# The last 96 hidden features of an MLP on Trainium2, computed as three strips of 32 in TensorE's column groups and row groups

## The chip, the cores and the metric

The kernel runs on one core of a Trainium2 chip. The metric is the time of one execution in microseconds of device time, lower is better. Engines are named as in the profile: PE is TensorE (matrix multiply; PEld is its loading of weights), DVE is VectorE, ACT is ScalarE, POOL is GpSimd, SP is SyncE, which here only issues DMAs.

## The reference

Four layers follow one another on x of 2048 tokens by 512 features, bfloat16: a long-convolution layer A, an MLP B, and both again with the same weights.

```
x = A_q
x = x + A(layernorm(x))
x = x + B(layernorm(x))
x = x + A(layernorm(x))
x = x + B(layernorm(x))

A(q) = q * (causal_conv(kv, ssm_k) + kv * ssm_D)     # kv = shift(k) * v, by FFT of length 4096
B(x) = gelu(layernorm(x) @ w1 + b1) @ w2 + b2        # w1 is 512 x 1376, w2 is 1376 x 512
```

The factor that multiplies q in A depends on k and v alone, so it is the same for both A layers and is computed once. The hidden width is F = 1376 = 10 x 128 + 96.

## The kernel before

**Two parts.** The first part of the program (to about 100 us) computes the factor of A by Fourier transforms written as matmuls, and in its last stretch begins the MLP of the first four token tiles. Its pieces stand in an order written out by hand, the string `ORDER`: each word is the name of a piece, the engine that takes it (P, D, A, G for GpSimd, S for SyncE's DMAs) and the slots it uses. `_Plan.write` emits the pieces in that order. The second part (from about 101 us to the end) is a loop written in plain code, each engine taking its instructions in the order in which they are emitted.

**The loop.** The 2048 tokens are 16 tiles of 128, in 4 groups of `GT = 4` tiles (512 tokens). The loop takes n = 0 to 7: groups 0 to 3 for the first MLP and 0 to 3 again for the second. For each n:

- `mm1(n)` makes the hidden activations `hT`, features on partitions, 512 tokens along the free axis. For each of `FT = 11` feature tiles, 4 matmuls (one for each 128 of the 512 inputs, `ct`) add up in a PSUM buffer `ph` of pool `ps2`, and ACT applies gelu with the bias `B1` into `hT`. The last feature tile has only `FL = 96` features.
- `mm2(n)` multiplies back: for each token tile i, 11 matmuls of 512 columns (one for each feature tile) add up in an accumulator `po` of pool `ps3`. The eleventh contracts over 97 rows: 96 features and a row of ones, which meets b2 in a 97th row of the weights `W2t`. The first two token tiles stop after 8 feature tiles and are finished later, so that ACT has time for the last gelus.
- `done(i)` on DVE adds the accumulator to the tokens `x_t`; for n of 4 and more the result is sent out.
- `prep(n + 2)`, two turns ahead, has four steps on DVE, two of which end with one small POOL instruction (`scale`): `c0` statistics of the first layernorm (POOL: `scale`), `c1` the normalised tokens times the factor of A, added to `x_t`, `c2` statistics of the next norm (POOL: `scale`), `c3` the norm applied into `lnx`, and a transposing DMA on SP from `lnx` into `lnT[n % 3]`, from which `mm1(n + 2)` reads. `c0` and `c1` are emitted ahead of `mm1(n)`, `c2` after the first 16 matmuls of `mm2(n)`, `c3` after `done(1)`.

For n = 0 the hidden activations are made within the hand-written order, by the pieces `M0a` to `M2c` (token tiles 0, then 1, then 2 and 3 together), and `prep(1)` and `prep(2)` both run beside `mm2(0)`.

**Memory.** One big tile, `arena`, holds nearly all data; `place` gives each array an offset in it, and arrays that live at different times share a place. `Ft` holds the table of the first transform stage. The dependency tracking of the framework puts in the waits.

Of the kernel before, what the change touches and what calls it, by code (L numbers as in the profile page):

```python
# [18 lines left out]
lSK.S wm2.P2 bS.P2 wm0.P1 bSe.A dg0.D dg1.A dg2.A lk0.S lk1.S lh1.S kT0.P2 bSK.P1 bSKe.A kT0e.D kT1.P0 kT2.P3 lh113.S lb1.S lx0.S kT1e.D kT2e.A kT3.P1 wm1.P0 bB.P2 bBe.A lv0.S s00.A lv1.S kT3e.D kv10.P3 kvm10.D kv00.P1 U1S0.P30 kv01.P2 kvm00.D U1S1.P1 U0S0.P01 U1S0e.D lK01.S kg0.G kv11.P3 lK00.S kg1.G U0S0e.A kvm01.D U0S1.P0 s01.G U0S1e.A U0S3.P2 U1S1e.D kvm11.D U0S3e.A kv20.P1 kd0.P0 lK11.S lK10.S kvm20.D kd0e.A U1S3.P3 U0S2.P2 U1S3e.A U0S2e.D KS11.P0 KS11e.A KS01.P1 KS30.P3 KS01e.A lW.S KS00.P2 KS00e.A KS30e.D KS10.P0 KS31.P1 KS10e.D kv21.P3 kvm21.D KS31e.A kd4.P1 kd4e.A KS20.P0 KS21.P2 KS20e.A KS70.P1 KS21e.D KS51.P3 KS41.P0 KS70e.A KS51e.A KS60.P2 KS60e.A KS41e.D KS40.P1 KS61.P3 KS40e.D lX.S KS71.P0 KS50.P2 U1S2.P1 KS71e.D KS61e.A KS50e.A U1S2e.A U2S0.P32 U2S0e.D K25.P0 K25e.A K27.P2 K24.P1 K24e.A K23.P3 K21.P0 K21e.A K27e.D K26.P2 U2S1.P1 K26e.A K23e.D U2S1e.D K20.P3 K28.P0 K20e.A K22.P2 K22e.A K212.P1 K28e.D K215.P3 K215e.A lM.S K212e.D sa1.S sb1.S sa0.S K214.P0 K29.P2 K29e.A K213.P1 U0T0.P3 K214e.D K213e.A K210.P0 K210e.A sb0.S K211.P2 U0T1.P1 s02.D K211e.A U2S3.P0 U0T0e.D U2S3e.A U0T1e.D ka1.G kg2.G ka2.G kg3.G X00.P30 ka3.G kgm.G U3S0.P21 U3S0e.D U2S2.P1 X00e.A X01.P01 lH.S U2S2e.A U1T0.P3 U3S1.P2 T00.D0 U3S3.P1 X01e.A U1T1.P0 sb3.S U1T0e.D X10.P30 U3S1e.A U3S3e.A sa3.S X02.P22 T01.D1 X10e.A U2T0.P1 sb2.S U1T1e.D T10.D2 U3S2.P3 U2T0e.D X02e.A sa2.S X12.P01 V00.P2 U3S2e.A T02.D0 V10.P30 X12e.A X03.P10 V00e.A X03e.A V01.P0 V01e.A X20.P22 T12.D2 X20e.A U3T0.S V12.P1 X11.P01 X11e.A V10e.D lx.S V02.P3 U2T1.P2 T03.D1 X13.P00 T20.D2 V12e.A V02e.A T11.D0 V03.P1 U2T1e.D X13e.A V03e.A X30.P32 T13.D1 V11.P0 X30e.A V11e.D X23.P21 V13.P1 X23e.A U3T1.S V13e.A T30.D0 X22.P30 X22e.A T23.D1 V20.P01 X21.P22 ly.S X21e.A V20e.A V30.P12 X32.P31 T22.D2 T21.D0 X31.P20 V22.P0 X32e.A V21.P3 X31e.A V30e.D X33.P12 V22e.A Z01.S Z00.S X33e.A V23.P2 T32.D2 V23e.A T31.D0 V32.P0 V31.P1 T33b.D1 V33b.P2 T33a.D2 V31e.D Z11.S Z10.S V21e.A V32e.A V33a.P3 Z03.S V33ae.A TC0a.P0 TC0b.P1 Z13.S TC0ae.A TC0be.A w4.S V33be.D TD0b.P3 TD0a.P0 TD0ae.D TC3.P2 TD0be.A Y00.P0 Y01.P3 Y00e.A Y01e.A TC3e.D g00.D w1.S Z02.S TC1.P1 TC1e.A g01.D h00.D Y02.P2 Y32.P0 TC2.P3 Y02e.A h01.D Y32e.A Y10.P1 Y10e.A p00.G w3.S b00.D g02.D p01.G LT0.P2 LT0e.A Y12.P0 Y12e.A M0b.P1 M0be.A TC2e.A h02.D M0a.P2 b01.D LT1.P1 Y30.P0 LT1e.A p02.G b02.D LT2.P3 LG1.D LT2e.D M1a.P1 M0ae.A M1ae.A M1b.P2 M1be.A M2a.P3 M2ae.A M2b.P1 M2be.A M2c.P2 M2ce.A Y30e.A Z12.S w2.S Y20.P3 Y22.P1 Y20e.A Y22e.A  # L19
# [85 lines left out]
def kernel(ctx: ExitStack, tc: tile.TileContext, A_q, A_k, A_v, A_shift_k, A_ssm_k, A_ssm_D,  # L105
# [9 lines left out]
    FL = F - (FT - 1) * P  # L115
    TOK = "(p nt) d -> p nt d"
# [58 lines left out]
    B1 = const.tile([P, FT], F32, name="B1")  # L175
# [88 lines left out]
    W2t = place("W2t", [P, FT, D], 75 * K)  # L264
# [3 lines left out]
    hT = place("hT", [P, FT, GT * P], 0)  # L268
    lnT = [place(f"lnT{i}", [P, GT, CT, P], o * K) for i, o in enumerate((12, 16, 20))]
    lnx = [place(f"lnx{i}", [P, GT, D], (96 + 4 * i) * K) for i in range(2)]  # L270
    tmpa = place("tmpa", [P, GT, D], 28 * K)
    ZV = at(100 * K, [[1, 8 * D]])

    with tc.tile_pool(name="ps", bufs=1, space=bass.MemoryType.PSUM) as ps:
# [93 lines left out]
        def bias(o):  # L368
            for ft in range(FT):
                nc.tensor.matmul(o[:, ft:ft + 1], b1r[:, ft * P:ft * P + P], one[0:1, 0:1], start=True, stop=True)  # L370
        _, sb = mm_evac("bB", 650, lS[1:2], bias, [FT], lambda: B1[:])
# [314 lines left out]
        def head(n, part, f0, f9, deps):  # L686
            a, b = UNITS[n]
            w = (b - a) * P

            def rows(ft):  # L690
                return P if ft < FT - 1 else FL

            def mms(it):
                o = view(pf[it["slot"]["ps"]], [f9 - f0, w])
                for ft in range(f0, f9):
                    m = rows(ft)
                    for ct in range(CT):
                        nc.tensor.matmul(o[0:m, ft - f0, :].rearrange("p (i t) -> p i t", t=P), W1t[:, ct, ft * P:ft * P + m],  # L698
                                         lnT[0][:, a:b, ct, :], start=ct == 0, stop=ct == CT - 1)
            pe = plan.add(f"M{n}{part}", {"P": 218 * (b - a) * (f9 - f0)}, deps, mms, take=["ps"])  # L700

            def gelu(it):
                o = view(pf[pe["slot"]["ps"]], [f9 - f0, w])
                for ft in range(f0, f9):
                    m = rows(ft)
                    nc.scalar.activation(hT[0:m, ft, a * P:b * P], o[0:m, ft - f0, :], AF.Gelu_apprx_tanh, bias=B1[0:m, ft:ft + 1])
# [18 lines left out]
    with tc.tile_pool(name="ps2", bufs=4, space=bass.MemoryType.PSUM, reuse_waits="tile") as ps2, \  # L725
            tc.tile_pool(name="ps3", bufs=4, space=bass.MemoryType.PSUM, reuse_waits="tile") as ps3:

        def mm1(n, a=0, b=GT, f0=0, f9=FT):
            lt = lnT[n % 3]
            for ft in range(f0, f9):  # L730
                m = P if ft < FT - 1 else FL
                ph = ps2.tile([P, GT * P], F32, name="ph", tag="ph")
                o = ph[0:m, a * P:b * P]
                for ct in range(CT):
                    nc.tensor.matmul(o.rearrange("p (i t) -> p i t", t=P), W1t[:, ct, ft * P:ft * P + m], lt[:, a:b, ct, :],  # L735
                                     start=ct == 0, stop=ct == CT - 1)
                nc.scalar.activation(hT[0:m, ft, a * P:b * P], o, AF.Gelu_apprx_tanh, bias=B1[0:m, ft:ft + 1])  # L737

        def prep(n):
# [19 lines left out]
            def c3():  # L759
                L.apply(ln, g, 0, GT)  # L760
                nc.sync.dma_start_transpose(lnT[n % 3].rearrange("p i ct t -> p (i ct) t"),
                                            ln.rearrange("p i d -> p (i d)"))
            return [c0, c1, c2, c3]

        def mm2(n, g, last, between):
            def part(i, po, f0, f9, a=0, b=D):
                for ft in range(f0, f9):
                    m = P if ft < FT - 1 else FL + 1
                    nc.tensor.matmul(po[:, a:b], hT[0:m, ft, i * P:(i + 1) * P], W2t[0:m, ft, a:b],  # L769
                                     start=ft == 0, stop=ft == FT - 1)  # L770

            def done(i, po, a=0, b=D):
                xs = x_t[:, GT * g + i, a:b]
                nc.vector.tensor_tensor(xs, po[:, a:b], xs, ALU.add)  # L774
# [10 lines left out]
            part(0, po0, FT - 3, FT)  # L785
            done(0, po0)
            part(1, po1, FT - 3, FT)
            done(1, po1)
            for f in between[1:]:
                f()  # L790
            po2 = acc()
            part(2, po2, 0, FT)
            done(2, po2)
            if n < 2 * NG - 1:
                po3 = acc()
                part(3, po3, 0, FT)
                done(3, po3)
            else:
                for a in (0, D // 2):
                    po3 = acc()  # L800
                    part(3, po3, 0, FT, a, a + D // 2)
                    done(3, po3, a, a + D // 2)

        NG = NT // GT
        with tc.manual_schedule(engines={ENG.PE, ENG.DVE, ENG.Activation, ENG.Pool, ENG.SP}):
            nc.gpsimd.memset(hT[FL:FL + 1, FT - 1, :], 1.0)
            for n in range(2 * NG):
# [8 lines left out]
                LG[1].scale(0, GT)  # L816
                for f in one_[1:] + pr[:1]:
                    f()
# [31 lines left out]
```

## Time and profile before

| | before |
|---|---|
| time, median of 3 runs | 249.34 us (249.3 to 249.93) |
| time of the profiled execution | 249.34 us |
| span of its profile, first to last instruction | 247.6 us |
| mean granted TensorE clock | 0.997 |
| PE busy | 236.1 us, 95% of the span, 1918 matmuls |
| DVE busy | 171.9 us, 69% |
| ACT busy | 145.1 us, 59% |
| POOL busy | 54.5 us, 22%, 50 instructions |

The profile has a page (busy times, the span in 40 slices, the chain of work that ended last, groups of instructions by line) and views that can be asked of its trace: the timeline of an engine, the instructions of one line, the waits, the engines' busy time in given stretches. The duration of a matmul in these rows includes its way through the array; successive matmuls overlap, so what a matmul costs in a stream is read from the distance between starts. In a form such as "128\*96 128x512" the first pair is rows and columns of the array that the weights fill, the second is the moving operand: 128 partitions by 512 columns.

### The profile page before, as it was taken

To read this page: it belongs to the slowest core of one execution; us is meant where nothing else is said; L and a number is where in the kernel's file an instruction comes from. 1 tells how busy PE (TensorE), PEld (TensorE's weight loads), DVE (VectorE), ACT (ScalarE), POOL (GpSimd) and SP (SyncE) were. 2 spreads that over 40 slices of the span, in tenths; PEclk is the share of its full clock that TensorE was granted. 3 is DMA by queue.
4 is the path that set the end of the run, shared out by engine and by line. 5 is a ranking of instruction groups with operands and counts; after the bars stand their busy time and mean duration, and the time that the engine had idled before them with its cause. 6 is when DMAs were issued, how large, how long until landed. Compare 5 with 4: busy or idle time off the path is not lost.

```text
span 247.6 us, 4783 instructions
## 1 busy us (share of the span) xinstructions
PE 236.1 (95%) x1918; PEld 146.4 (59%) x1929; DVE 171.9 (69%) x315; ACT 145.1 (59%) x218; POOL 54.5 (22%) x50
## 2 busy tenths in 40 slices
PE   4999999899999999999999999999999999999994
PEld 2689877699998688444444444444444444444443
DVE  1467899999997988878889898956956961021022
ACT  5596899899999899707406506505605604704800
POOL 2789999400000221111101111011011010000000
PEclk9999999999999999999999999999999999999998
DMA  6999994946999990040601204013016016011011
GB/s 244 351 292 173 264 437 192 394 175 120 218 254 179 282 260 5 0 85 1 87 0 38 47 3 85 0 23 63 3 44 127 0 45 127 1 42 42 3 42 42
DMA packets 50816, 29.65 MB, mean 120 GB/s; under 512 B 44675, under 2 KB 48488, under 8 KB 49258
## 3 DMA queue, kind: packets, MB, share of 16 engines
q1 hardware_dynamic: 50642, 29.21, 45.7%
q8 instruction: 15, 0.25, 0.4%
q10 hardware_dynamic: 152, 0.14, 0.2%
q14 instruction: 7, 0.06, 0.1%
HBM read 16.23 MB, written 2.10 MB: 74 GB/s over the span
## 4 chain that ended last, share of the span: by engine, by line
PE 72%; DVE 9%; ACT 9%; DMA 5%; issue 2%; POOL 0%; ACTq 0%; DVEq 0%; POOLq 0%
PE po L769 31%; PE ph L735 27%; ACT arena L215 3%; DMA arena<-in_A_v_dram 3%; ACT xb L215 3%; PE p L521 3%; DVE arena L217 3%; ACT ZT L215 2%; DMA arena<-in_A_ssm_D_dram 2%; PE p L698 2%; PE p L303 2%; DVE arena L254 2%; PE p L403 1%; PE p L335 1%; PE p L575 1%
## 5 line engine op out<-in xcount | busy, mean ns | idle before, releaser
L737 ACT ACTIVATE arena<-ph,B 128x512 bf16<-128x512 f32 (+1 forms) x77 | 52.9, 687 | 78.6 <-PE ph L735 78.6
L769 PE MATMUL po<-arena 128*128 128x512 bf16 (+2 forms) x356 | 77.1, 372 | 0.4
L735 PE MATMUL ph<-arena 128*128 128x512 bf16 (+1 forms) x308 | 67.6, 379 | 0.0
L769 PEld LDWEIGHTS <-arena 128*128 128x128 bf16 (+1 forms) x363 | 35.4, 98 | 40.7
L774 DVE TENSOR_TENSOR arena<-po,arena 128x512 bf16<-128x512 f32 (+1 forms) x33 | 21.6, 672 | 44.6 <-PE po L769 44.5
L735 PEld LDWEIGHTS <-arena 128*128 128x128 bf16 (+1 forms) x308 | 30.8, 100 | 35.9
L215 ACT ACTIVATE arena<-p 128x1024 bf16<-128x1024 f32 (+7 forms) x44 | 40.6, 1005 | 3.6 <-PE p L383 1.2
L249 POOL TENSOR_TENSOR lrsm<-lrsm,mhalf 128x4 f32<-128x4 f32 (+2 forms) x10 | 9.1, 910 | 92.3 <-DVE lrsm L243 89.5
L237 DVE BATCH_NORM_STATS2 lstm<-arena 128x6 f32<-128x512 bf16 x32 | 20.0, 681 | 0.2
L215 ACT ACTIVATE ZT<-p 128x1024 bf16<-128x1024 f32 (+1 forms) x18 | 17.9, 1040 | 1.9 <-PE p L303 1.7
L566 DVE TENSOR_TENSOR T<-xb,arena 128x2048 bf16<-128x2048 bf16 (+1 forms) x17 | 18.9, 1153 | 0.0
L254 DVE TENSOR_SCALAR arena<-arena,lmvg,lrsg 128x512 bf16<-128x512 bf16 x32 | 12.9, 465 | 7.3 <-POOL lrsg L249 7.3
L249 POOL TENSOR_TENSOR lrsg<-lrsg,mhalf 128x4 f32<-128x4 f32 x8 | 8.1, 1012 | 44.6 <-DVE lrsg L246 44.6
L237 DVE BATCH_NORM_STATS2 lstg<-arena 128x6 f32<-128x512 bf16 x28 | 17.2, 677 | 0.0
L575 PE MATMUL p<-arena,T 128*128 128x128 bf16 x256 | 16.2, 219 | 0.6 <-ACT ZT L215 0.3
L215 ACT ACTIVATE xb<-p 128x1024 bf16<-128x1024 f32 x16 | 16.3, 1059 | 0.6 <-PE p L551 0.6
L217 DVE COPY arena<-p 128x2048 bf16<-128x2048 bf16 (+3 forms) x12 | 12.3, 1031 | 5.1 <-PE p L439 3.3
L575 PEld LDWEIGHTS <-T 128*128 128x128 bf16 x256 | 14.8, 98 | 1.1 <-issue 0.7
L453 POOL TENSOR_TENSOR T<-arena,SK 128x2048 bf16<-128x2048 bf16 (+3 forms) x4 | 15.0, 3760 | 1.3 <-ACT SK L215 1.1
L254 DVE TENSOR_SCALAR arena<-arena,lmvm,lrsm 128x512 bf16<-128x512 bf16 x32 | 11.5, 416 | 2.8 <-POOL lrsm L249 2.8
L217 DVE CAST arena<-p 128x1024 bf16<-128x1024 f32 x11 | 12.9, 1217 | 0.3
L217 DVE CAST ZT<-p 128x1024 bf16<-128x1024 f32 (+1 forms) x11 | 12.8, 1170 | 0.4 <-ACT arena L215 0.2
(80 smaller groups left out, 249.5 us busy)
## 6 DMA issues: line engine op xcount, KB each, us to landing
arena<-arena SPq DMA_DIRECT2D x8, 512.0 KB, 5.6
arena<-in_A_k_dram SPq DMA_DIRECT2D x2, 1024.0 KB, 6.2
arena<-in_A_v_dram SPq DMA_DIRECT2D x2, 1024.0 KB
arena<-in_A_ssm_k_dram SPq DMA_DIRECT2D x4, 512.0 KB, 12.1
arena<-tabM SPq DMA_DIRECT2D x1, 2048.0 KB
out_dram<-arena SPq DMA_DIRECT2D x15, 128.0 KB, 1.7
arena<-in_A_q_dram SPq DMA_DIRECT2D x1, 1536.0 KB, 6.8
arena<-in_B_w_dram SPq DMA_DIRECT2D x1, 1376.0 KB, 6.7
```

Of the source, the lines that this page charges most:

```text
L215: nc.scalar.activation(dst, src, AF.Copy)
L217: nc.vector.tensor_copy(dst, src)
L237: nc.vector.bn_stats(self.st[:, i, 0, :], x_t[:, GT * g + i, :] if src is None else src[:, i, :])
L249: nc.gpsimd.tensor_tensor(self.rs[:, a:b], self.rs[:, a:b], mhalf[:, a:b], ALU.pow)
L254: nc.vector.tensor_scalar(out=dst[:, i, :], in0=xs, scalar1=self.mv[:, i, 0:1], scalar2=self.rs[:, i:i + 1], op0=ALU.subtract, op1=ALU.mult)
L453: nc.gpsimd.tensor_tensor(m[:, t:NT, :], kn[:, 0:NT - t, c3], sk(t, NT - t), ALU.mult)
L566: eng.tensor_tensor(view(Tb[it["slot"]["T"]], [2, n, CW]), x2, kk, ALU.mult)
L575: nc.tensor.matmul(o[:, i, :], T[:, r, i, :], Mt[:, ka + i, 1 - r, :], start=r == 0, stop=r == 1)
L735: nc.tensor.matmul(o.rearrange("p (i t) -> p i t", t=P), W1t[:, ct, ft * P:ft * P + m], lt[:, a:b, ct, :], start=ct == 0, stop=ct == CT - 1)
L737: nc.scalar.activation(hT[0:m, ft, a * P:b * P], o, AF.Gelu_apprx_tanh, bias=B1[0:m, ft:ft + 1])
L769: nc.tensor.matmul(po[:, a:b], hT[0:m, ft, i * P:(i + 1) * P], W2t[0:m, ft, a:b], start=ft == 0, stop=ft == FT - 1)
L774: nc.vector.tensor_tensor(xs, po[:, a:b], xs, ALU.add)
```

## The change

The 96 hidden features that do not fill a feature tile are taken out of the loops over feature tiles, and cut into `FS = 3` strips of 32 features.

- **First product, `tail_mm`.** For each strip s and each `ct`, four matmuls, one for each token tile i of the group, have the same 32 columns of `W1t` as weights and 128 tokens as moving operand. The result of tile i goes to PSUM partitions 32i to 32i + 31, that is to column group i of the array. So 48 matmuls of 128 columns stand where 4 of 512 columns stood. In the loop they come first in `mm1`, ahead of the ten full feature tiles; for n = 0 they are a new piece `M3` (with `M3e` on ACT) at the end of `ORDER`, after the last products of A.
- **Gelu, `tail_gelu`.** Three ACT instructions of 128 partitions by 128 write `hq`: on partitions 32i to 32i + 31 the strip's features of token tile i. `B1` has 13 columns in place of 11, the last three with each strip's bias repeated four times; they are made by 22 small matmuls in place of 11.
- **Second product, `tail` in `mm2`.** For each strip, four matmuls, one for each token tile, contract over 32 rows: partitions 32i to 32i + 31, that is row group i of the array. They write four accumulators, which are all taken at the start of `mm2`. So 12 matmuls of 512 columns stand where 4 stood (for n = 7 the last tile's accumulator is in two halves). They come after the first 16 matmuls of `mm2`. The weights for them, `W2q`, hold the last 96 rows of w2 four times, once for each group of 32 partitions, loaded by four DMAs where one was.
- **b2.** The row of ones goes, and with it the POOL memset. b2 is loaded into `Ft`, repeated on all partitions, and POOL adds it to `x_t` (`add_b2`): for group 0 in four instructions of 512 columns behind the `scale` of `prep(1)`, for the others in one of 2048 columns at the end of `c3`. The adds are eight groups' worth in all.

At the end of the string `ORDER` stand two words more, `M3.P0 M3e.A`; the rest of it is as before. The diff without that line:

```
+    FS = FL // 32
...
-    B1 = const.tile([P, FT], F32, name="B1")
+    B1 = const.tile([P, FT + FS - 1], F32, name="B1")
...
+    hq = place("hq", [P, FS, P], 10 * K)
+    W2q = place("W2q", [P, FS, D], 136 * K)
     ZV = at(100 * K, [[1, 8 * D]])
+
+    def tail_mm(o, lt):
+        for s in range(FS):
+            f0 = (FT - 1) * P + 32 * s
+            for ct in range(CT):
+                for i in range(GT):
+                    nc.tensor.matmul(o[32 * i:32 * i + 32, s, :], W1t[:, ct, f0:f0 + 32], lt[:, i, ct, :], start=ct == 0, stop=ct == CT - 1)
+
+    def tail_gelu(o):
+        for s in range(FS):
+            nc.scalar.activation(hq[:, s, :], o[:, s, :], AF.Gelu_apprx_tanh, bias=B1[:, FT - 1 + s:FT + s])
...
-            for ft in range(FT):
+            for ft in range(FT - 1):
                 nc.tensor.matmul(o[:, ft:ft + 1], b1r[:, ft * P:ft * P + P], one[0:1, 0:1], start=True, stop=True)
-        _, sb = mm_evac("bB", 650, lS[1:2], bias, [FT], lambda: B1[:])
+            for s in range(FS):
+                f0 = (FT - 1) * P + 32 * s
+                for i in range(GT):
+                    nc.tensor.matmul(o[32 * i:32 * i + 32, FT - 1 + s:FT + s], b1r[:, f0:f0 + 32], one[0:1, 0:1], start=True, stop=True)
+        _, sb = mm_evac("bB", 650, lS[1:2], bias, [FT + FS - 1], lambda: B1[:])
...
-        w3 = load("w3", W2t[0:FL, FT - 1, :], B_w2[(FT - 1) * P:F, :], 96 << 10, wd)
-        w4 = load("w4", W2t[FL:FL + 1, FT - 1, :], apf(B_b2, 0, [[D, 1], [1, D]]), 1024, wd)
+
+        def load_tail(it):
+            for i in range(GT):
+                nc.sync.dma_start(W2q[32 * i:32 * i + 32, :, :], apf(B_w2, (FT - 1) * P * D, [[D, 32], [32 * D, FS], [1, D]]))
+        w3 = plan.add("w3", {"S": 600}, wd, load_tail, dma=("copy", 384 << 10))
+        w4 = load("w4", Ft[:, 0:D], apf(B_b2, 0, [[0, P], [1, D]]), 2 ** 17, wd)
...
-            for part, f0 in enumerate(range(0, FT, step)):
-                head(n, "abc"[part], f0, min(f0 + step, FT), [lt[n], w1])
+            for part, f0 in enumerate(range(0, FT - 1, step)):
+                head(n, "abc"[part], f0, min(f0 + step, FT - 1), [lt[n], w1])
+        m3 = plan.add("M3", {"P": 640}, [lt[n] for n in range(3)] + [w1], lambda it: tail_mm(view(pf[it["slot"]["ps"]], [FS, P]), lnT[0]),
+                      take=["ps"])
+        plan.add("M3e", {"A": 600}, [m3, sb] + wd, lambda it: tail_gelu(view(pf[m3["slot"]["ps"]], [FS, P])), free=[(m3, "ps")])
...
-        def mm1(n, a=0, b=GT, f0=0, f9=FT):
+        def mm1(n):
             lt = lnT[n % 3]
-            for ft in range(f0, f9):
-                m = P if ft < FT - 1 else FL
+            ph = ps2.tile([P, GT * P], F32, name="ph", tag="ph")
+            pt = ph[:, 0:FS * P].rearrange("p (s t) -> p s t", t=P)
+            tail_mm(pt, lt)
+            tail_gelu(pt)
+            for ft in range(FT - 1):
...
+        def add_b2(g, a, b):
+            xs = x_t[:, GT * g + a:GT * g + b, :]
+            b2 = apf(Ft, 0, [[Ft.shape[1], P], [0, b - a], [1, D]])
+            nc.gpsimd.tensor_tensor(xs, xs, b2, ALU.add)
...
                                             ln.rearrange("p i d -> p (i d)"))
+                add_b2(g, 0, GT)
             return [c0, c1, c2, c3]
...
+            def tail(parts):
+                for s in range(FS):
+                    for i, po, a, b in parts:
+                        rs = slice(32 * i, 32 * i + 32)
+                        nc.tensor.matmul(po[:, 0:b - a], hq[rs, s, :], W2q[rs, s, a:b], start=s == 0 and i > 1, stop=False)
...
-            po0, po1 = acc(), acc()
-            part(0, po0, 0, FT - 3)
-            part(1, po1, 0, FT - 3)
+            parts = [(i, acc(), 0, D) for i in range(GT)]
+            if n == 2 * NG - 1:
+                parts[3:] = [(3, parts[3][1], 0, D // 2), (3, ps2.tile([P, GT * P], F32, name="ph", tag="ph"), D // 2, D)]
+            for i, po, *_ in parts[:2]:
+                part(i, po, 0, 8)
             for f in between[:1]:
                 f()
...
+            tail(parts)
+            for i, po, *_ in parts[:2]:
+                part(i, po, 8, FT - 1)
+                done(i, po)
...
-            nc.gpsimd.memset(hT[FL:FL + 1, FT - 1, :], 1.0)
...
                 one_ = prep(1)
                 LG[1].scale(0, GT)
+                for i in range(GT):
+                    add_b2(0, i, i + 1)
                 for f in one_[1:] + pr[:1]:
                     f()
                 mm2(0, 0, False, pr[1:])
```

Two places in the order of instructions matter below. The first is POOL's queue from the last `scale` of the hand-written part on. In these rows `lrsm` and `lrsg` are the scales of the two norms and `mhalf` their exponent; L249 before and L250 after are the same line of `scale`. Before:

```order
L249 TENSOR_TENSOR lrsm0_110<-lrsm0_110,mhalf_77 128x2 [waits DVE_49]
L806 MEMSET arena_64 1x512 [waits DMAHW3_49,Activation_49,Pool_49]
L249 TENSOR_TENSOR lrsg1_107<-lrsg1_107,mhalf_77 128x4 [waits DVE_49,Pool_49]
L249 TENSOR_TENSOR lrsm1_113<-lrsm1_113,mhalf_77 128x4 [waits DVE_49]
L249 TENSOR_TENSOR lrsg0_104<-lrsg0_104,mhalf_77 128x4 [waits DVE_49]
L249 TENSOR_TENSOR lrsm0_110<-lrsm0_110,mhalf_77 128x4 [waits DVE_49]
```

After, where L765 is `add_b2`:

```order
L250 TENSOR_TENSOR lrsm0_110<-lrsm0_110,mhalf_77 128x2 [waits DVE_49]
L250 TENSOR_TENSOR lrsg1_107<-lrsg1_107,mhalf_77 128x4 [waits DVE_49]
L765 TENSOR_TENSOR arena_64<-arena_64,Ft_73 128x512 [waits DMAHW4_49,DMAHW5_49,PE_49,Pool_49]
L765 TENSOR_TENSOR arena_64<-arena_64,Ft_73 128x512 [waits PE_49] x3
L250 TENSOR_TENSOR lrsm1_113<-lrsm1_113,mhalf_77 128x4 [waits DVE_49]
L765 TENSOR_TENSOR arena_64<-arena_64,Ft_73 128x2048 [waits DMAHW6_49,DVE_49,PE_49]
L250 TENSOR_TENSOR lrsg0_104<-lrsg0_104,mhalf_77 128x4 [waits DVE_49]
L250 TENSOR_TENSOR lrsm0_110<-lrsm0_110,mhalf_77 128x4 [waits DVE_49,Pool_49]
```

Four adds now stand right behind the first `lrsg1` scale, which releases `c1` of `prep(1)` on DVE, and ahead of the `lrsm1` scale of its `c2`; one add of 2048 columns stands between that and the `lrsg0` scale of `prep(2)`.

The second place is TensorE's queue in `mm2(1)`, where it comes to the accumulators of token tiles 2 and 3. Before, between the first two tiles' last matmuls and the third tile's first (L769 is the one line of all these matmuls):

```order
L769 LDWEIGHTS arena_64 [waits Activation_49]
L769 MATMUL po_1870<-arena_64 128x512
...
L769 MATMUL po_1871<-arena_64 128x512
L769 LDWEIGHTS arena_64
L769 MATMUL po_1911<-arena_64 128x512 [waits DVE_49]
```

After, from the sixteenth matmul of `mm2(1)` on (L797 is a full feature tile, L804 a strip):

```order
L797 MATMUL po_1980<-arena_64 128x512
L804 LDWEIGHTS arena_64
L804 MATMUL po_1979<-arena_64 128x512
...
L804 MATMUL po_1980<-arena_64 128x512
...
L804 MATMUL po_1981<-arena_64 128x512 [waits DVE_49]
L804 LDWEIGHTS arena_64
L804 MATMUL po_1982<-arena_64 128x512 [waits DVE_49]
```

The first matmul of the third accumulator, with its wait for DVE to have emptied that buffer in the turn before, stood at the 23rd matmul of `mm2`, and now stands at the 19th, the fourth accumulator's at the 20th.

More of the change, by code (lines that the diff above doesn't have):

```diff
@@ L263 @@
     W1t = place("W1t", [P, CT, F], 64 * K)
-    W2t = place("W2t", [P, FT, D], 75 * K)
+    W2t = place("W2t", [P, FT - 1, D], 75 * K)
     KSW = place("KSW", [P, NA, D], 64 * K)
@@ L767, in part @@
                 for ft in range(f0, f9):
-                    m = P if ft < FT - 1 else FL + 1
-                    nc.tensor.matmul(po[:, a:b], hT[0:m, ft, i * P:(i + 1) * P], W2t[0:m, ft, a:b],
-                                     start=ft == 0, stop=ft == FT - 1)
+                    nc.tensor.matmul(po[:, 0:b - a], hT[:, ft, i * P:(i + 1) * P], W2t[:, ft, a:b], start=ft == 0 and i < 2,
+                                     stop=ft == FT - 2)
+            def tail(parts):
[3 more added lines that the diff above has]
+                        nc.tensor.matmul(po[:, 0:b - a], hq[rs, s, :], W2q[rs, s, a:b], start=s == 0 and i > 1, stop=False)
             def done(i, po, a=0, b=D):
                 xs = x_t[:, GT * g + i, a:b]
-                nc.vector.tensor_tensor(xs, po[:, a:b], xs, ALU.add)
+                nc.vector.tensor_tensor(xs, po[:, 0:b - a], xs, ALU.add)
                 if last:
```

36 lines of the change are left out of this document (9 added, 27 removed).

## The prediction

> **What bounds the kernel now.** I read the busy times by stretch first, then the chain that ended last, then the timeline. The stretches (columns: us, then busy us of PE, PEld, DVE, ACT, POOL, with counts) show where the edit lies:
>
> ```profile
> 50.00:88.00 38.00, 36.60 (x548) 33.15 (x548) 36.12 (x43) 36.85 (x42) 1.25 (x2) 1.00 0.94 203
> 101.20:234.71 133.51, 133.14 (x612) 61.08 (x618) 85.70 (x206) 54.91 (x80) 13.10 (x13) 1.00 0.20 40
> ```
>
> From 101.20 us on PE is busy without a gap (133.14 of 133.51 us); DVE, ACT and POOL have room. Earlier, three engines share the bound. The chain in order of time (start, us, what) says the same of the loop:
>
> ```profile
> 101.37 9.51 PE po L769 x44
> 110.88 9.50 PE ph L735 x44
> ```
>
> A turn is 44 matmuls of `mm1` and 44 of `mm2`, 9.50 / 44 = 0.216 us each. So in the loop every us that TensorE gains or loses counts in full, and other engines only if TensorE waits for them.
>
> **TensorE's part.** The matmuls that go are these (columns: busy us, mean ns of one):
>
> ```profile
> L735 PE MATMUL ph<-arena 128*96 128x512 bf16 x28 | 7.2, 379 | 0.0
> L769 PE MATMUL po<-arena 97*128 97x512 bf16 x31 | 11.8, 381 | 0.0
> ```
>
> Per turn that is 4 x 0.216 = 0.86 us in `mm1` and 0.86 in `mm2`. In their place come 48 matmuls of 128 columns and 12 of 512. If four neighbours in different groups run at once, these are 12 rounds of 128 columns and 3 of 512. The trace has no column groups, but it has row groups: the two halves of L403 (64 rows each).
>
> ```profile
> 43.27 0.27 PE L403 MATMUL p<-arena,Wt 64*128 64x256 bf16 x1
> 43.48 1.22 PE L335 MATMUL p<-IDt,ZT 128*128 128x128 bf16 x16
> 44.63 0.28 PE L403 MATMUL p<-arena,Wt 64*128 64x256 bf16 x1
> 44.63 0.39 PE L403 MATMUL p<-arena 64*128 64x256 bf16 x2
> 44.75 0.37 PE L403 MATMUL p<-arena,Wt 64*128 64x256 bf16 x2
> 44.86 0.38 PE L403 MATMUL p<-arena 64*128 64x256 bf16 x2
> 45.61 1.22 PE L335 MATMUL p<-IDt,ZT 128*128 128x128 bf16 x16
> 46.66 0.60 PE L303 MATMUL p<-Ft,arena 128*128 128x256 bf16 x4
> ```
>
> A pair starts at one instant (44.63 twice) and the next 0.11 us later, about what a single matmul of 256 columns takes (L303: (0.60 - 0.27) / 3 = 0.11). Row groups do run at once. The rows also price the change of grouping: L335's 16 full matmuls take 44.63 - 43.48 = 1.15 us where the split L403 follows, 1.05 (46.66 - 45.61) where the full L303 does, so 0.10 us to enter; a pair at 43.27 should be followed at 43.38, and L335 starts at 43.48, so 0.10 to leave. Each tail is entered and left once: 0.20 us per tail, four changes a turn.
>
> `mm2`'s tail, by these rows: 3 x 0.216 + 0.20 = 0.85 us against 0.86, no gain. For `mm1`'s tail I have two rows for its rounds:
>
> ```profile
> 19.08 1.79 PE p L521 x32
> 10.70 0.42 PE L370 MATMUL p<-one,arena 1*128 1x1 bf16 x11
> L370 PE MATMUL p<-one,arena x11: 158/158/173, 10.7 to 11.0; 1*128 1x1 bf16 x11
> ```
>
> L521 streams 128 columns in 1.79 / 32 = 0.056 us, so 12 full rounds are 0.67 us. L370 has next to nothing to stream, and still takes (0.42 - 0.158) / 10 = 0.026 us for a load and a matmul in one group; if that holds across groups, 48 x 0.026 = 1.25 us. With no overlap it is 48 x 0.056 = 2.69. I take 0.67, since L403's pairs start together; that is nearest in kind. Tail: 0.67 + 0.20 = 0.87 against 0.86.
>
> So a turn comes out even: 0.01 x 7 for `mm1`, -0.01 x 8 for `mm2`. For n = 0 it is worse, since `M3` is new work after a stretch that waits for DVE:
>
> ```profile
> 94.68 4.96 PE L698 MATMUL p<-arena 128*128 128x256 bf16 x44 [0.19 <-DVE arena L217]
> ```
>
> What leaves before 94.68 us only lengthens that wait; behind it 4 matmuls of about 0.11 us go, and 0.87 comes: +0.44 us. TensorE's sum is about +0.4 us.
>
> The Trainium skill ("TensorE: Matmul & The Clock Gate", "The mechanism" under Part 3) says that weight loads overlap matmuls in flight only where the row group differs. In `mm1`'s tail every matmul uses all rows; what that would do is a rival below.
>
> **ACT, SP and the bias.** Three gelus of 128 columns replace one of 512:
>
> ```profile
> 91.43 6.76 ACT L706 ACTIVATE arena<-p,B 128x128 bf16<-128x128 f32 x23
> 100.88 2.86 ACT L215 ACTIVATE arena<-p 128x1024 bf16<-128x1024 f32 x3
> ```
>
> 6.76 / 23 = 0.29 each, 0.88 in place of 0.68, beside 8.6 us of matmuls: nothing. For n = 0 ACT ends its evacuations at 103.74, `M3e` at 104.6; `mm2(0)`'s tail comes 16 x 0.216 after 101.2 + 0.44, at 105.1: covered by 0.5 us. Three more loads on SP, 0.57 us each, push the transpose and the big w2 load behind them by 1.7 us:
>
> ```profile
> 82.61 0.57 SPq L279 DMA_DIRECT2D arena<-in_B_w_dram  x1
> 86.17 0.58 SPq L279 DMA_DIRECT2D arena<-in_B_w_dram  x1
> arena<-in_B_w_dram SPq DMA_DIRECT2D x1, 1376.0 KB, 6.7
> ```
>
> w2 then lands near 86.2 + 1.7 + 6.7 = 94.6, needed at 101.2: nothing.
>
> ```profile
> 14.53 2.36 DVE L527 TENSOR_TENSOR arena<-p,arena 128x1024 bf16<-128x1024 f32 x2 [2.90 <-DMA arena<-in_A_v_dram]
> ```
>
> Eleven more 1-column matmuls in the bias, near 11 us, cost 0.3 us and a change of grouping, ahead of a stretch in which DVE, and TensorE behind it, wait for a load until 14.53 us anyway: nothing.
>
> **b2 on POOL.** This is where I expect the loss.
>
> ```profile
> 36.75 0.93 POOL L455 TENSOR_TENSOR T<-kh,SK 128x384 bf16<-128x384 bf16 x1
> 37.75 4.07 POOL L460 TENSOR_TENSOR T<-T,T 128x2048 bf16<-128x2048 bf16 x1
> 41.90 4.09 POOL L464 TENSOR_TENSOR arena<-arena,T 128x2048 bf16<-128x2048 bf16 x1
> 40.53 3.48 DVE L217 CAST arena<-p 128x1024 bf16<-128x1024 f32 x3
> 43.93 3.19 DVE L254 TENSOR_SCALAR arena<-arena,lmvg,lrsg 128x512 bf16<-128x512 bf16 x4
> 95.22 1.38 DVE L254 TENSOR_SCALAR arena<-arena,lmvg,lrsg 128x512 bf16<-128x512 bf16 x4 [0.59 <-POOL lrsg L249]
> 96.63 1.23 DVE L751 TENSOR_TENSOR arena<-arena 128x2048 bf16<-128x2048 bf16 x1
> 97.89 1.23 DVE L752 TENSOR_TENSOR arena<-arena 128x2048 bf16<-128x2048 bf16 x1
> ```
>
> An add of 2048 columns takes 4.07 us, one of 512 between 1.02 (a quarter) and 1.2 (from the 0.93 for 384): I take 1.1. While POOL's L464 ran, DVE's L254 took 3.19 us in place of 1.38: it stood still until POOL ended at 45.99, while casts from PSUM before it went on. The Trainium skill ("SBUF — State Buffer", "Who interferes with whom") calls this an exclusive lock, held for a whole instruction, also against DVE instructions with two SBUF inputs; the trace shows it for L254, and no row here for L751 or L752.
>
> In a steady turn the add starts after `c3`, when DVE next does `done(2)`, `done(3)` (from PSUM) and statistics, so it meets little. For n = 0 the four adds run from 95.2 us, just when DVE has `c1` of `prep(1)`. `c1` begins with four L254s; if POOL and DVE take turns, each of them waits for one add, 4.4 us. What that delays:
>
> ```profile
> 104.64 1.93 SPq L761 DMA_TRANSPOSE arena<-arena  x1
> 107.56 1.01 POOL L249 TENSOR_TENSOR lrsg<-lrsg,mhalf 128x4 f32<-128x4 f32 x1 [4.36 <-DVE lrsg L246]
> 119.06 1.28 DVE L774 TENSOR_TENSOR arena<-po,arena 128x512 bf16<-128x512 f32 x2
> 110.72 9.66 PE L735 MATMUL ph<-arena 128*128 128x512 bf16 x44
> DMA to landing us min/median/max: 4.2/4.3/5.1
> ```
>
> This transpose feeds `mm1(1)`. It lands at 104.64 + 4.3 = 108.94; TensorE asks at 110.72, so 1.78 us spare, 2.22 with `M3`'s 0.44. A delay of 4.4 leaves a stall of 2.2 us. If DVE, once let in, keeps its turn, it loses one add, 1.2 us, and nothing stalls. I take the stall, because each DVE instruction gives the port up at its end and a POOL add is always waiting; bounds 0 and 2.5 (4 x 1.17). The next add, of 4.07 us behind `c3` (109.0 to 113.1), then holds the `lrsg0` scale, due at 107.56 + 4.4, for 1.1 us. DVE's `done(3)` of turn 0 ends at 120.34 + 4.4 + 1.1 = 125.8; `mm2(1)`'s tail asks for that accumulator at 110.72 + 2.64 + 9.5 + 16 x 0.216 = 126.3: just free.
>
> Sum: 0.4 + 2.2 = +2.6 us. The profiled execution took 249.34 us (span 247.6 and 1.74 around it), equal to the median of the runs: 251.9 us.
>
> **The rivals.** About 0.3%, 0.75 us, is what a measurement of this kernel can tell from no change.
>
> - *DVE keeps its turn, no stall.* For: 1.78 us of slack. Against: nothing shows who wins. +0.4, 249.7 us. Chance 0.20.
> - *Loads set the pace in column groups*, 0.026 us each. For: L370. Against: L403's pairs. `mm1` +0.59 x 7, n = 0 +1.02, so +5.0; the stall shrinks to 1.6: 254.4 to 256.0 us. Chance 0.22.
> - *Column groups don't overlap at all.* `mm1`: 2.69 + 0.20 - 0.86 = +2.03, x 7, n = 0 +2.46: +16.5, no stall since TensorE is late itself: 266 us. Against: a load overlaps the matmul ahead of it in L521, with all rows. Chance 0.13. The Trainium skill's rule on row groups, above, would give this case.
> - *Faster: changes of grouping cost less inside the loop*, where loads queue up behind long matmuls. There are 7 x 2 + 2 + 16 = 32 changes; each 0.01 us less gives 0.32. Without a stall, below 0.064 us per change the kernel gains more than 0.75 us; at zero it is 0.4 - 3.2 = -2.8, 246.5 us. Against: two rows at 0.10. Chance 0.10.
>
> **The numbers.** The forecast, even turns and one stall, has 0.35: 251.9 us. The range runs from 248.0, which takes in half of the faster case, to 257.0, above the pace of loads with the stall; it leaves out the no-overlap case and the best of the gain. Faster 0.10; within 0.3% the no-stall case, 0.20; slower 0.70.
>
> **What would show it.** In the profile after: `mm1`'s tail 0.87 us from its first start to the first full tile (1.45 for the pace of loads, 2.9 for no overlap), `mm2`'s 0.85; a wait of TensorE for a DMA ahead of `mm1(1)` of about 2 us, and `c1` of `prep(1)` on DVE near 8 us long in place of 3.9. I am wrong if turns after the second differ from 19.0 us by over 0.3, or if DVE delays TensorE again later.

## The result, and the profile after

The changed kernel takes 250.13 us (median of 12 runs, 249.66 to 250.74), the kernel before 249.40 (12 runs). The ratio is 1.0029, 95% interval 1.0018 to 1.0039: slower by 0.73 us, just at what a measurement can tell. The forecast was +2.6 us. The profiled execution of after took 250.16 us, +0.82 on the one of before.

The first rows of the page of after (span; busy us and share, instructions), to be held against the table of before:

```profile
span 248.4 us, 5638 instructions
PE 236.3 (95%) x2331; PEld 146.1 (59%) x2350; DVE 176.2 (71%) x315; ACT 146.5 (59%) x232; POOL 87.0 (35%) x60
```

PE is as busy as before, with 421 more weight loads (2350 against 1929), one for each matmul; POOL has 32.5 us more. The timeline of PE in after, from the end of the first part to the second turn (start, us, what, and the idle time before it with what ended it):

```profile
101.63 0.85 PE L282 MATMUL p<-arena 128*32 128x128 bf16 x48 [0.62 <-ACT arena L216]
102.41 3.63 PE L797 MATMUL po<-arena 128*128 128x512 bf16 x15
105.97 0.82 PE L804 MATMUL po<-arena 32*128 32x512 bf16 x12
106.73 5.14 PE L797 MATMUL po<-arena 128*128 128x512 bf16 x23
112.20 0.85 PE L282 MATMUL ph<-arena 128*32 128x128 bf16 x48 [0.33 <-DMA arena<-arena]
112.99 8.81 PE L758 MATMUL ph<-arena 128*128 128x512 bf16 x40
121.63 3.62 PE L797 MATMUL po<-arena 128*128 128x512 bf16 x15
125.18 0.83 PE L804 MATMUL po<-arena 32*128 32x512 bf16 x12
125.94 5.14 PE L797 MATMUL po<-arena 128*128 128x512 bf16 x23
131.22 0.85 PE L282 MATMUL ph<-arena 128*32 128x128 bf16 x48
```

(A matmul is missing from some rows: x15 and x23 are 16 and 24 in the kernel.) The same place in before:

```profile
101.20 9.67 PE L769 MATMUL po<-arena 128*128 128x512 bf16 x44
```

Three things are to be read here. A whole turn, from one strip block of `mm1` to the next, is 131.22 - 112.20 = 19.02 us; before it was 2 x 9.50 = 19.0. With the strips ahead of it, `mm2(0)` starts at 102.41 in place of 101.20, 1.21 us late; the row of the strips shows 0.62 us of idle time until ACT was done. And `mm1(1)` starts at 112.20 in place of 110.72, 1.48 late, and only a small part of that is a wait for the transposing DMA. The row says 0.33, but the record missing from x23 may be part of that idle time, so the wait is better read from starts: from the start of `mm2` to the next strips it is 112.20 - 102.41 = 9.79 us here and 131.22 - 121.63 = 9.59 in the next turn, where nothing waits. The wait costs 0.20.

Starts of two traces can be compared like this because both profiled executions lie at their kernel's median. Otherwise the first part alone can differ by several tenths: in `cols_serial` below, which is the same kernel up to `M3`, `M3` starts at 100.85 and not at 101.63, in an execution of 249.66 us.

The timeline of DVE in after, and below it that of POOL, show where the transpose is held up:

```profile
95.15 4.71 DVE L255 TENSOR_SCALAR arena<-arena,lmvg,lrsg 128x512 bf16<-128x512 bf16 x4 [0.53 <-POOL lrsg L250]
99.90 1.23 DVE L779 TENSOR_TENSOR arena<-arena 128x2048 bf16<-128x2048 bf16 x1
107.80 2.46 DVE L238 BATCH_NORM_STATS2 lstg<-arena 128x6 f32<-128x512 bf16 x4
110.58 1.52 DVE L247 TENSOR_SCALAR lrsg<-lmvg 128x4 f32<-128x4 f32 x1
```

```profile
95.08 4.64 POOL L765 TENSOR_TENSOR arena<-arena,Ft 128x512 bf16<-128x512 bf16 x4
108.02 4.06 POOL L765 TENSOR_TENSOR arena<-arena,Ft 128x2048 bf16<-128x2048 bf16 x1 [1.55 <-PE po L797]
```

The four normalising instructions of `c1` take 4.71 us in place of 1.38, during POOL's four adds, and the next DVE instruction starts at 99.90 in place of 96.63: 3.27 late. The transpose that follows is as late on SP's queue (before: 104.64):

```profile
107.91 1.76 SPq L789 DMA_TRANSPOSE arena<-arena  x1
```

The last instructions on DVE, of before and of after (from the timelines of the last 5 us), hold a surprise:

```profile
244.03 0.42 DVE L774 TENSOR_TENSOR arena<-po,arena 128x256 bf16<-128x256 f32 x1 [0.78 <-PE po L769]
```

```profile
245.50 0.42 DVE L808 TENSOR_TENSOR arena<-ph,arena 128x256 bf16<-128x256 f32 x1 [0.67 <-PE ph L797]
```

The last sum is 1.47 us late, as `mm1(1)` was: nothing was lost or won in the seven turns between. But the span grew by 0.8 only. From the last sum to the end of the span before had 247.6 - 244.0 = 3.6 us, after has 248.4 - 245.5 = 2.9. So the change costs 1.5 us, and 0.65 of it comes back behind the last useful instruction. The experiments had to explain three numbers: 1.21 for the first strips, 0.20 for the stall, and -0.65 for the end.

### The profile page after: what moved, and what is told of

Same layout as the page of the kernel before. It is cut to its first block, busy times and chain, and to the rows that moved or that the text cites. A ratio compares the mean times of both kernels' runs of the same rounds, so it can differ in the third digit from the quotient of the medians.

```text
span 248.4 us, 5638 instructions
## 1 busy us (share of the span) xinstructions
PE 236.3 (95%) x2331; PEld 146.1 (59%) x2350; DVE 176.2 (71%) x315; ACT 146.5 (59%) x232; POOL 87.0 (35%) x60
## 4 chain that ended last, share of the span: by engine, by line
PE 53%; DMA 2%; DVE 1%; issue 1%
PE ph L758 25%; PE po L797 24%; PE ph L282 2%; PE po L804 2%; DMA arena<-arena 2%; DVE arena L255 1%; PE ph L797 0%; DVE arena L808 0%; PE ph L804 0%; DVE lstg L238 0%
## 5 line engine op out<-in xcount | busy, mean ns | idle before, releaser
L797 PE MATMUL po<-arena 128*128 128x512 bf16 (+1 forms) x305 | 68.8, 376 | 0.4
L758 PE MATMUL ph<-arena 128*128 128x512 bf16 x280 | 61.6, 379 | 0.0
L760 ACT ACTIVATE arena<-ph,B 128x512 bf16<-128x512 f32 x70 | 48.1, 687 | 11.6 <-PE ph L758 11.1
L797 PEld LDWEIGHTS <-arena 128*128 128x128 bf16 x330 | 31.6, 98 | 38.1 <-issue 3.2
L808 DVE TENSOR_TENSOR arena<-po,arena 128x512 bf16<-128x512 f32 (+1 forms) x32 | 20.7, 677 | 40.8 <-PE po L797 35.6
L758 PEld LDWEIGHTS <-arena 128*128 128x128 bf16 x280 | 26.8, 98 | 32.1
L286 ACT ACTIVATE arena<-ph,B 128x128 bf16<-128x128 f32 x21 | 6.2, 365 | 66.7 <-PE ph L282 66.7
L250 POOL TENSOR_TENSOR lrsm<-lrsm,mhalf 128x4 f32<-128x4 f32 (+2 forms) x10 | 9.1, 910 | 91.0 <-DVE lrsm L244 91.0
L765 POOL TENSOR_TENSOR arena<-arena,Ft 128x2048 bf16<-128x2048 bf16 (+1 forms) x11 | 33.1, 3016 | 16.2 <-DVE arena L255 14.7
L255 DVE TENSOR_SCALAR arena<-arena,lmvg,lrsg 128x512 bf16<-128x512 bf16 x32 | 16.1, 565 | 7.3 <-POOL lrsg L250 7.3
```

The costliest lines, as they stand in the source:

```text
L255: nc.vector.tensor_scalar(out=dst[:, i, :], in0=xs, scalar1=self.mv[:, i, 0:1], scalar2=self.rs[:, i:i + 1], op0=ALU.subtract, op1=ALU.mult)
L758: nc.tensor.matmul(ph[:].rearrange("p (i t) -> p i t", t=P), W1t[:, ct, ft * P:ft * P + P], lt[:, :, ct, :], start=ct == 0, stop=ct == CT - 1)
L760: nc.scalar.activation(hT[:, ft, :], ph[:], AF.Gelu_apprx_tanh, bias=B1[:, ft:ft + 1])
L765: nc.gpsimd.tensor_tensor(xs, xs, b2, ALU.add)
L797: nc.tensor.matmul(po[:, 0:b - a], hT[:, ft, i * P:(i + 1) * P], W2t[:, ft, a:b], start=ft == 0 and i < 2, stop=ft == FT - 2)
L808: nc.vector.tensor_tensor(xs, po[:, 0:b - a], xs, ALU.add)
```

## The experiments

Eight kernels ran, the first four on one chip, the others on a second; every ratio is to the kernel before on the same chip.

**The adds alone, on the kernel before.** b2 goes through POOL, the last feature tile stays in one piece with 96 rows.

```diff
+                add_b2(g, 0, GT)
...
-                    m = P if ft < FT - 1 else FL + 1
+                    m = P if ft < FT - 1 else FL
...
-            nc.gpsimd.memset(hT[FL:FL + 1, FT - 1, :], 1.0)
...
+                for i in range(GT):
+                    add_b2(0, i, i + 1)
```

> The kernel before with b2 alone changed: POOL adds it to the tokens as in the kernel after, the last feature tile stays one tile of 96 (no strips). My theory: the four adds of group 0 hold up DVE's c1 of prep(1) by 3.3 us, the transpose for mm1(1) lands at 112.1 us, TensorE is ready at 110.7 and waits 1.4 us; the turns stay at 19.0 us. The last matmul ends 1.4 us later than before. If the shorter end of the program after its last DMA (0.6 us in the profile after) comes with POOL's ten more instructions, the time is 250.2 us; if not, 250.8. Rival, the loss is in the strips: no wait at mm1(1), 249.4 us.

Measured: 250.18 us against 249.28, 1.0038 (1.0024 to 1.0053). Its DVE and PE timelines:

```profile
95.52 4.71 DVE L254 TENSOR_SCALAR arena<-arena,lmvg,lrsg 128x512 bf16<-128x512 bf16 x4 [0.53 <-POOL lrsg L249]
```

```profile
89.26 2.63 PE L698 MATMUL p<-arena 128*128 128x128 bf16 x44 [1.13 <-DMA arena<-in_B_w_dram]
112.58 1.67 PE L735 MATMUL ph<-arena 128*128 128x512 bf16 x7 [0.36 <-DMA arena<-arena]
```

The 4.71 us are there again, with no strips in the kernel: the adds alone make them. The time came out as expected, the path only in part. The run has a wait for the load of w1, 1.13 us before 89.26, which neither before nor after has. Since TensorE had lost that much already, only 0.36 us of wait were left at `mm1(1)`. The transpose sets that start in either case. Why w1 came late is not explained; the profiled execution took 250.72 us, 0.54 more than the median of this kernel's runs, so the wait may belong to that execution alone.

**The strips without b2.** Both calls of `add_b2` are taken out of after.

> The kernel after without any add of b2 (the output lacks b2), so POOL has no adds. My theory: c1 of prep(1) takes 3.9 us again, mm1(1) doesn't wait for its DMA and starts 0.33 us earlier, at 111.9 us: 0.3 us off the kernel after, 249.8 us; if the shorter end of the program hangs on the number of POOL's instructions, it is lost here and the time is 250.4. Rival, POOL's adds cost DVE and so TensorE in every turn: over 1 us off, below 249.1.

Measured: 250.42 us, 1.0041 (1.0026 to 1.0055), not below after. The PE and DVE timelines:

```profile
101.66 0.85 PE L282 MATMUL p<-arena 128*32 128x128 bf16 x48 [0.62 <-ACT arena L216]
112.05 0.85 PE L282 MATMUL ph<-arena 128*32 128x128 bf16 x48
```

```profile
95.18 1.38 DVE L255 TENSOR_SCALAR arena<-arena,lmvg,lrsg 128x512 bf16<-128x512 bf16 x4 [0.53 <-POOL lrsg L250]
```

The four instructions are back at 1.38 us, and the wait for the DMA is gone, but `mm1(1)` starts only 0.15 us earlier, near the 0.20 that the wait cost: TensorE is late by the strips itself, the 0.62 for ACT still included. By the time alone one would say that b2 costs nothing. Yet this kernel's end is long again, 248.6 - 245.3 = 3.3 us.

**The wait for ACT.** `M3` needs the PSUM slot P0. It is held by the product `Y30`, whose evacuation `Y30e` stands in ACT's order behind the gelus `M2ae` to `M2ce`. Moved ahead of them, with the slots of `Y22` and `M3` exchanged, at the end of `ORDER`:

```diff
- M2a.P3 M2ae.A M2b.P1 M2be.A M2c.P2 M2ce.A Y30e.A Z12.S w2.S Y20.P3 Y22.P1 Y20e.A Y22e.A M3.P0 M3e.A
+ M2a.P3 Y30e.A M2ae.A M2b.P1 M2be.A M2c.P2 M2ce.A Z12.S w2.S Y20.P3 Y22.P0 Y20e.A Y22e.A M3.P1 M3e.A
```

> The kernel after with Y30e moved ahead of M2ae on ACT, and the PSUM slots of Y22 and M3 exchanged so that M3 finds its slot free. My theory: M3 starts 0.7 us earlier, but mm1(1) still starts when its transpose lands, at 112.1 us: TensorE's wait there grows from 0.33 to 1.0 us and the time stays at 250.1 us, within 0.2. Rival, M3's wait counts in full: 249.45 us.

Measured: 250.24 us, 1.0031 (1.0021 to 1.0042), no gain. On PE:

```profile
100.93 0.85 PE L282 MATMUL p<-arena 128*32 128x128 bf16 x48
112.27 0.85 PE L282 MATMUL ph<-arena 128*32 128x128 bf16 x48 [1.10 <-DMA arena<-arena]
```

The wait for ACT is gone and `M3` starts 0.70 us earlier; the wait for the transpose grows from 0.33 to 1.10 in the rows, and by starts from 0.20 to 0.96 (`mm2(0)` starts at 101.72). So in after two delays lie side by side in front of `mm1(1)`, TensorE's own and DVE's, nearly equally late. Taking away one shows the other.

**Both taken away:** `Y30e` moved and no adds.

> Both: M3 finds its slot free, and no add of b2 (the output lacks b2). My theory: mm1(1) starts at 111.2 us, 0.5 us after the kernel before, and every turn is 19.0 us; 1.0 us off the kernel after, 249.1 us with the short end of the program, 249.7 with the long one. So the two delays, of which neither alone is worth more than 0.3 us, are worth 1.0 together. Rival, the strips cost TensorE time in each turn: no less than 249.8 with the short end.

Measured: 249.67 us, 1.0009 (0.9998 to 1.0020), 0.6 us less than with `Y30e` moved alone, and it has the long end (last sum at 244.99, span 248.3: 3.3 us). In the profiled execution, 0.43 us above the median of the runs, `mm1(1)` starts at 111.69, later than expected, and without a wait.

**The end of the program.** The kernels with a long end are those with few POOL instructions. The queue from which the engines' instructions are fetched, as the DMA view shows it for the end of before, from 235 us on, and of after, in the same stretch:

```profile
q1 hardware_dynamic: 720, 0.52, 6.4%
q14 instruction: 1, 0.01, 0.1%
```

```profile
q1 hardware_dynamic: 720, 0.52, 6.4%
```

Before fetches a block of instructions there, after does not. Ten small POOL memsets of a tile that nothing reads, put into the kernel before, lengthen POOL's program:

```diff
+    spare = const.tile([P, 4], F32, name="spare")
...
+                nc.gpsimd.memset(spare[:], 0.0)
...
+            for _ in range(3):
+                nc.gpsimd.memset(spare[:], 0.0)
```

> The kernel before with ten small POOL memsets of a spare tile added (three at the loop's start, one at the end of each c3), so that POOL's program is ten instructions longer, as in the kernel after; nothing reads the tile. My theory: the stretch from the last DVE addition to the end of the program shrinks from 3.57 us towards the 2.94 of the kernel after, since its late POOL instruction is late by its place in POOL's program: 0.4 to 0.6 us faster than before, 248.8 us. Rival, the shorter end of the program has to do with the adds or the strips: 249.4 us, no change.

Measured: 248.96 us against 249.56, 0.9975 (0.9965 to 0.9985). Ten more instructions make the kernel before 0.6 us faster. Its span and last sum:

```profile
span 247.3 us, 4803 instructions
```

```profile
244.26 0.42 DVE L776 TENSOR_TENSOR arena<-po,arena 128x256 bf16<-128x256 f32 x1 [0.78 <-PE po L771]
```

The end is 3.0 us in place of 3.6, and the late fetch is gone. All three kernels with the late fetch (before and the two without b2) have an end of 3.3 to 3.6 us, all seven without it one of 2.9 to 3.1. The memsets alone did it, so the longer program of POOL shortens the end, without strips and without adds.

The traces also show where the time lies. After the last output POOL takes part in the closing of the program. Its two DRAIN instructions there, of before and of after (ns min/median/max, first and last start):

```profile
L845 POOLq DRAIN  x2: 78/126/173, 246.6 to 247.2; - x2
```

```profile
L873 POOLq DRAIN  x2: 34/56/77, 247.9 to 248.2; - x2
```

Between the two, POOL stands still in before: from the instruction ahead of the second DRAIN (246.70) to that DRAIN (247.19) it is 0.49 us, in after 0.13 (248.04 to 248.17). In the two kernels without b2 the pause comes two instructions later, 0.42 us (248.11 to 248.53) and 0.44 (247.76 to 248.20), where after has 0.08. Counted from the start of POOL's instructions as the trace lists them, it is the same place in all three, between the 68th and the 69th; the other seven list 80 or more and reach the 69th long before the end. So the place in POOL's program decides.

The fetch itself is not what the end waits for. Its packet starts at 247.88 us in before, 0.28 behind the end of the span, and 0.59 behind it in the two others; and the time outside the span is the same with it and without (1.74 us in before, 1.72 with the memsets). Pause and fetch come together, but what POOL does in the pause is not shown.

**The adds moved.** On top of `Y30e` moved, two of group 0's adds go behind a small POOL copy that waits for `c1` of `prep(1)`, the other two behind the add of group 1:

```diff
-                for i in range(GT):
-                    add_b2(0, i, i + 1)
-                for f in one_[1:] + pr[:1]:
-                    f()
+                one_[1]()
+                nc.gpsimd.tensor_copy(spare[:], x_t[:, GT:2 * GT, 0])
+                add_b2(0, 0, 2)
+                for f in one_[2:]:
+                    f()
+                add_b2(0, 2, GT)
+                pr[0]()
```

> The kernel after with M3 as in m3_early, and the adds of b2 for group 0 moved: those of two tiles start when DVE has finished c1 of prep(1) and run beside its statistics, the other two tiles follow the add of group 1. All is computed. My theory: no wait of TensorE ahead of mm1(1), which starts at 111.2 us, 1.0 us earlier than in the kernel after; 249.1 to 249.3 us, as fast as before, with the short end of the program. Rival, the moved adds hold up DVE at another place (the scale of prep(2), then the accumulators of mm2(1)): a wait there and no gain, 250.1.

Measured: 249.18 us, 0.9987 (0.9976 to 0.9997). On PE:

```profile
111.14 0.85 PE L283 MATMUL ph<-arena 128*32 128x128 bf16 x48
130.16 0.85 PE L283 MATMUL ph<-arena 128*32 128x128 bf16 x48
```

`mm1(1)` starts at 111.14 without a wait: 0.42 us behind before, near the prediction's price for `M3` (0.44). The adds are all still there. They cost only where they stood. Part of the ratio is the short end: against before with ten more POOL instructions, 248.96 us on the same chip, this kernel is not faster.

**One change of grouping less.** On top of that, in all turns but the last, the strips of `mm2(n)` move to its end, so that row groups are followed at once by the column groups of `mm1(n + 1)`. The four `done` come behind them, and for n = 0 the steps of `prep` that stood between the tiles too. From the edit:

```diff
+            if n < 2 * NG - 1:
+                for i, po, *_ in parts[:2]:
+                    part(i, po, 8, FT - 1)
...
+                for i, po, *_ in parts[2:]:
+                    part(i, po, 0, FT - 1)
+                tail(parts)
+                for i, po, *_ in parts:
+                    done(i, po)
```

> adds_moved, and the strips of mm2(n) moved to its end, so that the row groups of mm2(n) and the column groups of mm1(n + 1) follow each other directly (the last turn is as it was): three changes of grouping a turn in place of four. All is computed. My theory: a change costs 0.1 us, so a turn takes 18.9 us and seven turns gain 0.7: 248.5 us, faster than both. Rival, going from row groups to column groups costs as much as two changes, or the four additions at the end hold up DVE: 249.2 or more.

Measured: 248.52 us against 249.56, 0.9960 (0.9945 to 0.9975), faster than both kernels. On PE:

```profile
110.64 0.83 PE L805 MATMUL po<-arena 32*128 32x512 bf16 x12
111.39 0.85 PE L283 MATMUL ph<-arena 128*32 128x128 bf16 x48
112.18 8.81 PE L759 MATMUL ph<-arena 128*128 128x512 bf16 x40
129.55 0.83 PE L805 MATMUL po<-arena 32*128 32x512 bf16 x12
130.31 0.85 PE L283 MATMUL ph<-arena 128*32 128x128 bf16 x48
```

A turn is 130.31 - 111.39 = 18.92 us in place of 19.02, so a change of grouping costs 0.10 us in the loop too. From row groups straight to column groups (111.39 - 110.64 = 0.75 us, of which 3 x 0.216 are the strips) costs the same 0.10 as to the full array. Against before with ten more POOL instructions the gain is 0.4 us.

**The order within the column groups.** The two inner loops of `tail_mm` exchanged, so that the four matmuls of one column group are neighbours:

```diff
-            for ct in range(CT):
-                for i in range(GT):
+            for i in range(GT):
+                for ct in range(CT):
```

> The kernel after with the loops of tail_mm exchanged, so that the four matmuls of one token tile (one column group) stand next to each other, in place of four in different groups. My theory: matmuls overlap only with neighbours in other groups; in a strip 12 of 16 neighbours are now in one group and cost 0.056 us each, so a tail takes about 2.2 us in place of 0.79 and the kernel 11 us more, 261 us. Rival, each group has its own queue and takes its matmuls whatever their order: no change, 250.1.

Measured: 250.16 us, 1.0028 (1.0014 to 1.0042), as after.

```profile
111.42 0.89 PE L282 MATMUL ph<-arena 128*32 128x128 bf16 x48
112.24 8.81 PE L758 MATMUL ph<-arena 128*128 128x512 bf16 x40
```

48 matmuls take 0.82 us up to the first full tile, 0.79 in after. My theory that neighbours must lie in different groups fell.

## Why the prediction was wrong in size

Side and range were right, and so was the main mechanism: the turns are even, and the adds hold up `c1` of `prep(1)` and with it the transpose. The size was not: +0.73 us measured for +2.6. The step that failed is "each of them waits for one add, 4.4 us". `c1` lost 3.27 us. `mm1(1)` starts when the transpose lands, as long as TensorE is there first, so what is lost ahead of it is the delay less the 1.78 us spare: 4.4 - 1.78 = 2.62 by the prediction, 3.27 - 1.78 = 1.49 with the right delay, and 1.48 measured. The other part is a term that the sum lacked, the end of the program, which gave 0.65 back. Going by the prediction's own steps:

- **`mm1`'s and `mm2`'s tails: right.** Predicted 0.87 and 0.85 us. In after the strips of `mm1` take 132.01 - 131.22 = 0.79 from their first start to the first full tile. Ahead of them `mm2`'s 24 matmuls take 131.22 - 125.94 = 5.28 for 24 x 0.216 = 5.18, so 0.10 to enter: 0.89 in all. `mm2`'s are 125.94 - 125.18 = 0.76, and 0.10 to enter (125.18 - 121.63 = 3.55 for 16 x 0.216 = 3.46): 0.85. The two rows of 0.10 us per change of grouping, taken from another stage, held in the loop.
- **The rivals on the array: both fell.** No overlap would have shown 2.9 us per tail, the pace of loads 1.45. The rule of the Trainium skill ("TensorE: Matmul & The Clock Gate", "The mechanism" under Part 3), by which loads overlap only across row groups, does not hold for these column groups: every matmul uses all 128 rows, and the 48, with as many loads, run 4 at a time. The faster case fell with the same 0.10 us.
- **`M3`, "+0.44 us": mis-sized, 1.21 measured, without effect on the sum.** The work was priced about rightly (0.52 in `m3_early`, 0.42 in `adds_moved`). What was missed is the wait for the slot that `Y30` holds: `m3_early` takes it away and brings `M3` forward by 0.70 us. The prediction followed ACT's order behind `M3`, to `M3e` and the strips of `mm2(0)`, and not ahead of it, to who frees `M3`'s slot. Its own row had the answer: the first of ACT's three evacuations from 100.88 us on, 2.86 us for all, is `Y30e`, so the slot could not be free before about 101.8 us. Since the transpose came later still, this only turned time of the stall into lateness of TensorE.
- **"Each of them waits for one add, 4.4 us": right in kind, 3.27 measured.** POOL and DVE do take turns, and the rival in which DVE keeps its turn fell, though its 249.7 us lies nearest to the result. The four instructions one by one, in after and then in the kernel without the adds (ns min/median/max, first and last start):

```profile
L255 DVE TENSOR_SCALAR arena<-arena,lmvg,lrsg x4: 1231/1238/1244, 95.2 to 98.6; 128x512 bf16<-128x512 bf16 x4
```

```profile
L255 DVE TENSOR_SCALAR arena<-arena,lmvg,lrsg x4: 406/407/411, 95.2 to 96.2; 128x512 bf16<-128x512 bf16 x4
```

  Each waits for one add, and their starts are 1.16 us apart in place of 0.33. Four adds and four DVE instructions together take 4.71 us; the row of the adds in the same stretch has 4.64. The prediction put the four adds on top of DVE's 1.38 us, where DVE's instructions cost next to nothing between them: 4.64 - 1.38 = 3.26. `c1` as a whole took 7.2 us, for "near 8".
- **"A stall of 2.2": mis-sized, 0.20 measured.** The transpose starts at 107.91 and lands 4.2 to 4.3 us later, at about 112.2; the prediction had 113.3, from a delay of 4.4. Without a wait TensorE would have been there at 102.41 + 9.59 = 112.00; the prediction had 111.16, from a `M3` of 0.44. So TensorE is 1.28 late by itself and the stall adds 0.20. `m3_early` shows 0.96 of stall as soon as TensorE is early.
- **Later stalls: right, there are none.** POOL's `lrsg0` scale came at 112.18, when the next add had ended, and not 0.25 us behind the start of DVE's L247 as before, at 110.83: held for 1.35 us (the prediction: 1.1). L247 itself took 1.52 us beside that add. The next turns stayed even.
- **Not in the sum at all: the end, -0.65 us.** The prediction set the end of the work equal to the end of the span. `pool_count` shows that ten POOL memsets more are worth 0.6 us here. In the traces 0.5 of the 0.65 is in POOL's closing instructions; the rest lies ahead of them and is not explained.

Together: 1.28 + 0.20 - 0.65 = +0.83 us, the difference of the spans. The two terms in front of `mm1(1)` were forecast as 0.44 + 2.2 = 2.64, measured 1.48; the rest is the end.

## What to carry to other kernels

Where two chains meet ahead of the bound engine, price both, and for the engine's own chain look also at who frees the buffer that new work takes; taking away one of two equal delays gains next to nothing. An added instruction on an engine with room costs by where it stands: here the same adds cost 1 us beside a chain that is waited for, and nothing behind it. Before a difference of half a us is put down to an edit, compare the last useful instruction of both traces, not only the span: the end of the program has a length of its own, which the number of instructions on an idle engine can change. When such an end agrees with an event elsewhere in the trace, look which of the two comes first.

## What the runs showed of the hardware

- Matmuls in four column groups of 32 run four at a time, with loads of 128 rows each: 48 of 128 columns in 0.79 us with one change of grouping, the same when the four matmuls of one group are neighbours (0.82 us). The engine does not need them to be interleaved.
- Each change between full array, row groups and column groups costs 0.10 us, and row to column groups is one change, not two.
- A POOL add and DVE's normalising instruction alternate, one each, with DVE's time hidden between the adds (4.71 us for both, 4.64 for the adds in the same stretch). Statistics beside an add were not held (2.46 us as before), nor were sums from PSUM (two in 1.28 us, in the next turn, as before). The Trainium skill ("SBUF — State Buffer", "Who interferes with whom") states an exclusive lock that blocks for a whole instruction; the 1231 to 1244 ns agree.
- The end of the program is 2.9 to 3.1 or 3.3 to 3.6 us long, by the number of POOL instructions ahead of it. In the long ones 0.42 to 0.49 us lie between the starts of the 68th and the 69th instruction listed for POOL, where the same steps take 0.08 to 0.13 us in the short ones, and a block of instructions is fetched 0.28 to 0.59 us behind the end of the span. The Trainium skill ("Runtime: NRT & Kernel Launch", "Instruction fetch mechanics") calls the cost of a crossing into the next block of instructions "mostly hidden"; whether the pause is such a crossing, no run here shows, but its cost is not hidden.
